# Attention as a pipeline over units: the logits, maximum and Exp of the next unit stand ahead of the mix of this one

## The chip, the core and the metric

The kernel runs on one core of a Trainium2 chip, in one launch. The metric is the device time of that launch in microseconds (us). A core has a matrix engine (TensorE, PE in the profile; its weight loads are PEld), a vector engine (VectorE, DVE), a scalar engine (ScalarE, ACT), GpSimd (POOL) and a sync engine (SP) whose queue issues most of the DMAs. Each engine runs its own instructions in order; an instruction that waits for another engine or for a DMA holds up all that stand behind it on its engine. The same holds for the DMAs in SP's queue.

## What is computed

All in fp32, with S = 2048 tokens, D = 512 channels, F = 1792 hidden channels, 32 heads of 16 channels:

```python
g = sigmoid((x * gate_w).sum(-1, keepdims=True))
# a: attention, each token looks at 8 tokens: itself and those 2, 4, ..., 14 back
q, k, v = heads(x @ wqkv)
logits = einsum("bhsd,bhswd->bhsw", q, k[s - 2*w]) * 16 ** -0.5   # w = 0..7, masked before token 0
a = einsum("bhsw,bhswd->bhsd", softmax(logits), v[s - 2*w]) @ wo
# b: gated feed-forward
b = (gelu(x @ w_gate) * (x @ w_up)) @ w_down
out = g * a + (1 - g) * b
```

## The kernel before

**Halves.** A token looks back in steps of two, so even and odd tokens never meet in the attention. The kernel handles them as two halves, `par` 0 and then `par` 1, each of 1024 tokens. Each half first projects queries and keys (`project` and `project_one` for the first half, `keys` and `key_one` for the second, matmuls on L357 and L506) and values (`values`, L408), and then runs its feed-forward, `ffn(par)`, in 14 steps `f`. After the second feed-forward `out_first` and `finish` multiply the attention's output by `wo` (L1050) and write the result.

**TensorE.** Every fp32 matrix product is three products of rounded high and low parts (`hi`, `lo`), so each result takes three matmuls on a 128x512 tile. `gate_up` computes, for one step `f`, two blocks of gate and up in seven products instead of eight (L778, `p<-S,g` and `p<-A,g`); `down` multiplies the hidden values of two steps with `w_down` (L820). The results stand in eight PSUM banks: four named `acc`, four that rotate under the name `p`. ScalarE copies them out (`s`, `c`, `rt`), computes the Gelu (L870, L886) and rounds to the high parts (`hh`, L796); VectorE adds (L790), multiplies gate by up (L794) and makes the low parts (`hl`, L797) that `down` reads. Weights go through the same split: `combine` (L705) and `operands` (L729) on VectorE for one part, ScalarE and an adding DMA on POOL for the rest; `down_w` makes the parts of `w_down` (L766 for the low part of the first ones).

**The attention runs beside it, on VectorE.** Tokens lie on 128 partitions, eight successive tokens of a half to a partition. A unit is 128 channels (8 heads) of one half: four units in each half, eight in all, counted here from 0 to 7. Units 0 and 1 of a half use the first block of keys, units 2 and 3 the second. The generator `attention()` writes the work of a unit in four parts:

- `load_kq` loads keys and queries into the one buffer `kq` (three DMAs on SP, L553, L554, L550).
- `scores` runs four times: a product of 2048 elements (L569), and a sum over 16 channels (L572). A mask (L576) follows.
- `softmax`: maximum (L583), subtraction (L586), Exp on ScalarE (L588), sum (L589), reciprocal (L591), for the second half a product with the gate (L593), and a multiplication (L595). Beside the maximum an Exp of one element (L584, `ahead`) is issued on ScalarE, whose input is the maximum and whose output nobody reads.
- `mix` loads the values into the one buffer `v` (two DMAs on SP, L553 and L554) and runs four times: a product of 2048 elements (L609) and three additions (L613, L615, L617); after two of them a transpose (L622) and four stores to DRAM (`os`, L624). `channels` later reads these back, and splits them for the product with `wo` (L86 on ScalarE, L87 on VectorE).

There are two `lg` buffers for logits, one `kq`, one `v`, one `prod`, one `m` and one `tb`.

**What sets the order.** `attention()` yields after each instruction with a cost in microseconds. The feed-forward and the projections call `pull(budget)` at fixed places, which takes that many microseconds of work from the generator; a `need(...)` inside it waits until keys or values exist, and `need_o` at the end takes all that is left. The work so taken is given a lower priority. A planner with its own timing of every instruction then chooses the order on each engine, so a change of the generator moves instructions of all engines, also the matmuls. In the order that it makes now, the parts of the units follow one another on VectorE: scores, softmax and mix of one unit, then those of the next, with the feed-forward's instructions in between.

The loads of keys and queries of the next unit stand ahead of `mix`, if its keys are ready. Each half begins with a wait for its keys; the pause `LOAD` (4.0) stands in the generator behind a load that has nothing ahead of it.

Of the kernel before, what the change touches and what calls it, by code (L numbers as in the profile page):

```python
# [10 lines left out]
F32 = mybir.dt.float32  # L11
F32R = mybir.dt.float32r
AF = mybir.ActivationFunctionType
# [3 lines left out]
P = 128  # L17
S, D, F = 2048, 512, 1792
H, DH, W = 32, 16, 8
NT = S // P  # L20
NP = NT // 2
# [6 lines left out]
UC = 128  # L28
UH = UC // DH
# [4 lines left out]
LOAD = 4.0  # L34
# [10 lines left out]
def tile_gated_mix(ctx: ExitStack, tc: tile.TileContext, xt, wqkv, wff, wo, out):  # L45
    nc = tc.nc
    ctx.enter_context(nc.allow_non_contiguous_dma(reason="rows of 512 bytes"))
    pool = ctx.enter_context(tc.tile_pool(name="sb", bufs=1))
# [487 lines left out]
    LG = {}  # L536
# [15 lines left out]
    def load_slots(t, src):  # L552
        nc.sync.dma_start(t[:, :NP - 1], src[:S // 2].rearrange("(p j) d -> p j d", j=NP)[:, 1:])  # L553
        nc.sync.dma_start(t[:, NP - 1:], src[W:].rearrange("(p j) d -> p j d", j=NP))  # L554
# [22 lines left out]
                                op=OP.min)  # L577
        LG[par, u] = lg

    def softmax(par, u):  # L580
        lg = LG[par, u]
        m = pool.tile([P, UH, NP], F32, name="m")
        nc.vector.tensor_reduce(m, lg, axis=AX.X, op=OP.max)  # L583
        nc.scalar.activation(pool.tile([P, 32], F32, name="ahead")[:W, :1], m[:W, 0, :1], AF.Exp, scale=0.0)  # L584
        yield 0.7
        nc.vector.tensor_tensor(lg, lg, m[:, :, :, None].to_broadcast([P, UH, NP, W]), op=OP.subtract)  # L586
        yield 0.7
        nc.scalar.activation(lg, lg, AF.Exp, scale=DH ** -0.5)  # L588
        nc.vector.tensor_reduce(m, lg, axis=AX.X, op=OP.add)  # L589
# [5 lines left out]
        nc.vector.tensor_tensor(lg, lg, m[:, :, :, None].to_broadcast([P, UH, NP, W]), op=OP.mult)  # L595
        yield 0.7

    def mix(par, u, pause):
        lg = LG.pop((par, u))
        hh, c = divmod(u, 2)  # L600
        v = pool.tile([P, 2 * NP - 1, UC], F32, name="v")
        load_slots(v, VS[par, hh][c])
        yield pause
        tb = pool.tile([P, 2, BT * UC], F32, name="tb")
        for jj in range(0, NP, 2):
            if jj % BT == 0:
                o = pool.tile([P, 4, BT, 32], F32, name="o")
            prod = pool.tile([P, 2, W, UC], F32, name="prod")
            paced(nc.vector.tensor_tensor(prod.rearrange("p j w (h d) -> p (j w) h d", d=DH),  # L609
                                          spans(v, jj).rearrange("p j w (h d) -> p j w h d", d=DH),  # L610
                                          two_of(lg, jj)[:, :, :, None].to_broadcast([P, 2 * W, UH, DH]), op=OP.mult))
            yield 2.3
            nc.vector.tensor_tensor(prod[:, :, :4], prod[:, :, :4], prod[:, :, 4:], op=OP.add)  # L613
            yield 1.2
            nc.vector.tensor_tensor(prod[:, :, :2], prod[:, :, :2], prod[:, :, 2:4], op=OP.add)  # L615
            two = [prod[:, :, i].rearrange("p j (b c) -> p b j c", b=4) for i in range(2)]
            nc.vector.tensor_tensor(o[:, :, jj % BT:jj % BT + 2], *two, op=OP.add)  # L617
            yield 1.1

            if jj % BT == BT - 2:  # L620
                t = tb[:, jj // BT]
                nc.vector.transpose(t, o.rearrange("p b t c -> p (b t c)"))  # L622
# [12 lines left out]
    def need(*key):  # L635
        while key not in done:
            yield None

    def attention():
        units = [(0, u) for u in range(NU)] + [(1, u) for u in range(NU)]  # L640
        yield from need(0, 0)
        load_kq(0, 0)
        yield from scores(0, 0)
        yield from need(0, 1)
        scored, mixed = 1, False
        for i, un in enumerate(units):
            if scored == i:
                yield from need(un[0], un[1] // 2 * 2)
                load_kq(*un)
                yield LOAD  # L650
                yield from scores(*un)
                scored += 1
                mixed = False
            yield from need(un[0], 1)
            yield from softmax(*un)


            to = units[scored] if scored < len(units) else None
            ahead = to and (to[0], to[1] // 2 * 2) in done
            if ahead:  # L660
                load_kq(*to)
            yield from mix(*un, LOAD if mixed else 0.0)
            done.add((*un, "o"))
            mixed = not ahead
            if ahead:
                yield from scores(*to)
                scored += 1

    fill = attention()
    credit = [0.0]  # L670

# [567 lines left out]
```

## Time and profile before

| | |
|---|---|
| runs | 600.1, 600.45 and 601.49 us, median 600.45 |
| the profiled execution | 599.87 us |
| its span, first to last instruction | 598.1 us |
| mean granted TensorE clock | 0.998 |
| busy share of TensorE, VectorE, ScalarE, POOL | 99%, 89%, 70%, 15% |
| moved by DMA | 135.68 MB, mean 227 GB/s |

The profiled execution's own time is 1.77 us above its span, and 0.58 us below the median. A share is the engine's busy time over the span; the share of one stage can be another. Rows named by a line, such as L589, carry the line numbers of the kernel before. In the changed kernel the same instructions stand 3 to 13 lines further down (the sum is L592, the table of the Exp belongs to L587).

### The profile page before, as it was taken

How to read it: one execution, taken by the hardware profiler on the slowest of the kernel's cores; microseconds unless marked ns; L12 is line 12 of the kernel's file. 1: busy time of each engine (PE TensorE's matmuls, PEld its weight loads, DVE VectorE, ACT ScalarE, POOL GpSimd, SP SyncE). 2: the span in 40 equal slices, each digit the busy share in tenths (PEclk: the TensorE clock that was granted, in tenths of full speed). 3: DMA queues.
4: the chain of work that ended last, by engine and by line, in shares of the span. 5: the costliest groups of instructions: out<-in, count | busy, mean ns of one | idle time of the engine just before them, and what ended most of it. 6: DMA issues, size and time to landing. Idle time of an engine off the chain costs nothing.

```text
span 598.1 us, 8231 instructions
## 1 busy us (share of the span) xinstructions
PE 591.2 (99%) x2767; PEld 494.3 (83%) x2767; DVE 535.2 (89%) x626; ACT 417.4 (70%) x732; POOL 90.6 (15%) x113
## 2 busy tenths in 40 slices
PE   9999999999999999999999999999999999999997
PEld 7898878888888887888889888888888888888885
DVE  6959899998999969998889998999799979999882
ACT  6664666678877787778777666566877678696722
POOL 0140000111111111103001472111111111121200
PEclk9999999999999999999999999999999999999999
DMA  8795996968687775898899999688968896878815
GB/s 280 255 262 176 295 316 201 274 175 268 187 225 210 228 216 166 228 310 283 268 269 325 243 299 272 203 215 238 257 145 194 239 257 151 219 184 220 109 39 175
DMA packets 90520, 135.68 MB, mean 227 GB/s; under 512 B 8431, under 2 KB 54895, under 8 KB 90478
## 3 DMA queue, kind: packets, MB, share of 16 engines
q1 hardware_dynamic: 70686, 102.98, 52.0%
q0 software_dynamic: 15152, 29.70, 28.0%
q10 hardware_dynamic: 4640, 2.49, 1.4%
q8 instruction: 21, 0.34, 0.2%
q14 instruction: 21, 0.17, 0.1%
HBM read 69.83 MB, written 42.56 MB: 188 GB/s over the span
## 4 chain that ended last, share of the span: by engine, by line
PE 87%; DMA 6%; ACT 4%; DVE 1%; issue 1%; SPq 0%; ACTq 0%; DVEq 0%
PE p L778 41%; PE p L820 13%; PE acc L820 12%; PE p L1050 5%; PE acc L506 5%; PE p L357 2%; PE p L408 2%; PE acc L357 2%; PE acc L1050 2%; PE acc L408 2%; DMA kq<-kq 1%; DMA ks<-hh 1%; PE p L506 1%; DMA vs<-hh 1%; DMA kq<-ks 1%
## 5 line engine op out<-in xcount | busy, mean ns | idle before, releaser
L778 PE MATMUL p<-S,g 128*128 128x512 f32 x672 | 168.7, 389 | 0.7 <-ACT s L783 0.7
L778 PEld LDWEIGHTS p<-S,g 128*128 128x128 f32 x672 | 125.8, 188 | 27.5 <-ACT s L783 1.5
L778 PE MATMUL p<-A,g 128*128 128x512 f32 x504 | 125.1, 389 | 0.4 <-ACT c L886 0.4
L778 PEld LDWEIGHTS p<-A,g 128*128 128x128 f32 x504 | 94.4, 188 | 20.3 <-ACT c L886 0.8
L569 DVE TENSOR_TENSOR prod<-kq 128x2048 f32<-128x2048 f32 x32 | 72.8, 2277 | 4.3 <-DMA kq<-kq 3.6
L609 DVE TENSOR_TENSOR prod<-v,lg 128x2048 f32<-128x2048 f32 x32 | 72.9, 2280 | 0.7
L572 DVE TENSOR_REDUCE lg<-prod 128x128 f32<-128x2048 f32 x32 | 73.0, 2281 | 0.1
L820 PE MATMUL p<-d,hh 128*128 128x512 f32 x224 | 68.6, 390 | 0.4 <-ACT p L814 0.4
L736 POOL DMA_DIRECT2D g<-raw x28 | 24.1, 862 | 255.0 <-ACT g L733 149.6
L820 PE MATMUL acc<-d,hh 128*128 128x512 f32 x224 | 59.9, 389 | 0.0
L789 ACT ACTIVATE c<-p 128x512 f32<-128x512 f32 x56 | 33.5, 597 | 34.1 <-PE p L778 34.0
L820 PEld LDWEIGHTS p<-d,hh 128*128 128x128 f32 x224 | 42.0, 188 | 9.4 <-ACT p L814 0.8
L820 PEld LDWEIGHTS acc<-d,hh 128*128 128x128 f32 x224 | 42.0, 188 | 8.7
L797 DVE TENSOR_TENSOR hl<-c,hh 128x512 fp32r<-128x512 f32 x56 | 38.4, 686 | 6.4 <-ACT hh L796 6.2
L820 PE MATMUL p<-d,hl 128*128 128x512 f32 x112 | 42.9, 389 | 0.0
L794 DVE TENSOR_TENSOR c<-c 128x512 f32<-128x512 f32 x56 | 38.3, 683 | 4.5 <-ACT c L886 4.5
L790 DVE TENSOR_TENSOR c<-c,s 128x512 f32<-128x512 f32 x56 | 38.1, 685 | 3.3 <-ACT c L789 3.3
L783 ACT ACTIVATE s<-p 128x512 f32<-128x512 f32 x56 | 33.0, 594 | 11.3 <-PE p L778 10.1
L769 POOL DMA_DIRECT2D d<-r x23 | 19.7, 856 | 130.3 <-ACT d L768 107.2
L613 DVE TENSOR_TENSOR prod<-prod 128x1024 f32<-128x1024 f32 x32 | 39.0, 1220 | 0.2
L796 ACT ACTIVATE hh<-c 128x512 fp32r<-128x512 f32 x56 | 35.1, 627 | 5.1 <-DVE c L794 4.8
L833 ACT ACTIVATE rt<-p 128x512 f32<-128x512 f32 x48 | 28.5, 596 | 11.9 <-PE p L820 11.6
(215 smaller groups left out, 1004.6 us busy)
## 6 DMA issues: line engine op xcount, KB each, us to landing
g<-raw POOLq DMA_DIRECT2D x28, 512.0 KB, 6.1
raw<-wff SPq DMA_DIRECT2D x42, 256.0 KB, 4.3
ws<-g SPq DMA_DIRECT2D x14, 768.0 KB, 5.5
g<-ws SPq DMA_DIRECT2D x14, 768.0 KB, 7.0
r<-wff SPq DMA_DIRECT2D x28, 256.0 KB, 4.1
d<-r POOLq DMA_DIRECT2D x23, 256.0 KB, 7.1
v<-vs SPq DMA_DIRECT2D x8, 512.0 KB, 7.7
os<-tb SPq DMA_DIRECT2D x64, 64.0 KB, 4.8
```

The source lines that it names most:

```text
L506: LAST[:] = [nc.tensor.matmul(ps, x[:, ts], w, start=(start and kc == i == 0), stop=(kc == 1 and i == 2), skip_group_check=True)]
L569: paced(nc.vector.tensor_tensor(prod, spans(k, jj), q[:, jj:jj + 2, None, :].to_broadcast([P, 2, W, UC]), op=OP.mult))
L572: nc.vector.tensor_reduce(two_of(lg, jj), prod.rearrange("p j w (h d) -> p (j w) h d", d=DH), axis=AX.X, op=OP.add)
L609: paced(nc.vector.tensor_tensor(prod.rearrange("p j w (h d) -> p (j w) h d", d=DH), spans(v, jj).rearrange("p j w (h d) -> p j w h d", d=D ...
L613: nc.vector.tensor_tensor(prod[:, :, :4], prod[:, :, :4], prod[:, :, 4:], op=OP.add)
L778: LAST[:] = [nc.tensor.matmul(ps, w_, a_, start=(start and kc == 0 and n == 0), stop=(kc == 1 and n == 2), skip_group_check=True)]
L790: nc.vector.tensor_tensor(c, c, s, op=OP.add)
L794: nc.vector.tensor_tensor(ge, ge, up, op=OP.mult)
L796: nc.scalar.activation(hh_, ge, AF.Copy)
L797: nc.vector.tensor_tensor(hl_, ge, hh_.bitcast(F32), op=OP.subtract)
L820: LAST[:] = [nc.tensor.matmul(pp, a[:, ts], w, start=(i == 0 and n == 0 and gr == 0), stop=(i == 1 and n == 2), skip_group_check=True)]
L1050: LAST[:] = [nc.tensor.matmul(pa, a, b, start=(first and n == 0), stop=(last and n == 2), skip_group_check=True)]
```

## The change

`softmax` is cut in two. `exps` holds the maximum, the subtraction and the Exp; `shares` holds the sum, the reciprocal, the product with the gate and the multiplication. The one-element Exp `ahead` is gone. The load of the values moves out of `mix` into `load_values`.

The generator's order becomes: load of the values of unit u; scores and `exps` of unit u+1, if its keys are ready; the load of keys and queries of unit u+2, if those are ready; mix of unit u; `shares` of unit u+1. Where the keys of the next unit are not ready, the unit is done by itself as before, with the pause behind its load unless it is the first. This is so for unit 0 and for unit 4, the first units of the two halves. The last unit, 7, has no scores behind it.

```diff
-    def softmax(par, u):
+    def exps(par, u):
         lg = LG[par, u]
         m = pool.tile([P, UH, NP], F32, name="m")
         nc.vector.tensor_reduce(m, lg, axis=AX.X, op=OP.max)
-        nc.scalar.activation(pool.tile([P, 32], F32, name="ahead")[:W, :1], m[:W, 0, :1], AF.Exp, scale=0.0)
         yield 0.7
         nc.vector.tensor_tensor(lg, lg, m[:, :, :, None].to_broadcast([P, UH, NP, W]), op=OP.subtract)
         yield 0.7
         nc.scalar.activation(lg, lg, AF.Exp, scale=DH ** -0.5)
+
+    def shares(par, u):
+        lg = LG[par, u]
+        m = pool.tile([P, UH, NP], F32, name="m")
         nc.vector.tensor_reduce(m, lg, axis=AX.X, op=OP.add)
...
-    def mix(par, u, pause):
-        lg = LG.pop((par, u))
+    VT = {}
+
+    def load_values(par, u):
         hh, c = divmod(u, 2)
-        v = pool.tile([P, 2 * NP - 1, UC], F32, name="v")
+        VT[par, u] = v = pool.tile([P, 2 * NP - 1, UC], F32, name="v")
         load_slots(v, VS[par, hh][c])
-        yield pause
+
+    def mix(par, u):
+        lg, v = LG.pop((par, u)), VT.pop((par, u))
...
     def attention():
         units = [(0, u) for u in range(NU)] + [(1, u) for u in range(NU)]
...
+        def logits(i, wait):
+            if units[i] not in LG:
+                load_kq(*units[i])
+                if wait:
+                    yield LOAD
+            yield from scores(*units[i])
+            yield from exps(*units[i])
+            ready.append(i)
+
+        def share(i):
+            yield from need(units[i][0], 1)
+            yield from shares(*units[i])
+            shared.append(i)
+
         for i, un in enumerate(units):
-            if scored == i:
+            if i not in ready:
                 yield from need(un[0], un[1] // 2 * 2)
...
-            yield from need(un[0], 1)
-            yield from softmax(*un)
...
+                yield from logits(i, i > 0)
+            if i not in shared:
+                yield from share(i)
+            load_values(*un)
+            if keyed(i + 1):
+                yield from logits(i + 1, False)
+                if keyed(i + 2):
+                    load_kq(*units[i + 2])
+            yield from mix(*un)
             done.add((*un, "o"))
-            mixed = not ahead
-            if ahead:
-                yield from scores(*to)
-                scored += 1
+            if i + 1 in ready:
+                yield from share(i + 1)
```

More of the change, by code (lines that the diff above doesn't have):

```diff
@@ L640, in attention, with keyed @@
         units = [(0, u) for u in range(NU)] + [(1, u) for u in range(NU)]
[L641 to L645, printed above, removed]
+        ready, shared = [], []
+        def keyed(i):
+            return i < len(units) and (units[i][0], units[i][1] // 2 * 2) in done
+        def logits(i, wait):
[10 more added lines that the diff above has]
+            shared.append(i)
         for i, un in enumerate(units):
-            if scored == i:
+            if i not in ready:
                 yield from need(un[0], un[1] // 2 * 2)
-                load_kq(*un)
-                yield LOAD
-                yield from scores(*un)
-                scored += 1
-                mixed = False
-            yield from need(un[0], 1)
-            yield from softmax(*un)
-            to = units[scored] if scored < len(units) else None
-            ahead = to and (to[0], to[1] // 2 * 2) in done
-            if ahead:
-                load_kq(*to)
-            yield from mix(*un, LOAD if mixed else 0.0)
+                yield from logits(i, i > 0)
[7 more added lines that the diff above has]
+            yield from mix(*un)
             done.add((*un, "o"))
-            mixed = not ahead
-            if ahead:
-                yield from scores(*to)
-                scored += 1
+            if i + 1 in ready:
+                yield from share(i + 1)
     fill = attention()
```

## The prediction
> **What bounds the kernel now.** I read the page's busy times first, then TensorE's waits, then the chain that ended last.
>
> ```profile
> PE 591.2 (99%) x2767; PEld 494.3 (83%) x2767; DVE 535.2 (89%) x626; ACT 417.4 (70%) x732; POOL 90.6 (15%) x113
> ```
>
> ```profile
> PE p L72 <- DVE warm L69: 1.0, 1, 1.0
> PE p L778 <- ACT s L783: 0.7, 1, 0.7
> PE p L778 <- ACT c L886: 0.4, 1, 0.4
> PE p L820 <- ACT p L814: 0.4, 1, 0.4
> PE p L408 <- ACT p L415: 0.3, 1, 0.3
> ```
>
> ```profile
> 167.00 6.80 PE p L778 x30
> ...
> 591.36 2.73 PE p L1050 x12
> ```
>
> TensorE is busy for 591.2 of 598.1 us. All its waits for others come to 2.8 us, of which 1.0 is the start. The chain's row at 167.00 shows thirty matmuls in 6.80 us, 0.227 each, without a gap, and the last row shows the same rate at the very end (12 in 2.73). The change removes and adds no matmul: both built programs have 2767. So little can be gained: at most the waits behind the start, 1.8 us, that is 0.3%. Much can be lost wherever VectorE, ScalarE or a DMA comes late for a matmul.
>
> How late may they come? I looked at the end, where the last unit's results are split and multiplied with `wo`.
>
> ```profile
> 582.87 0.71 DVE L622 STREAM_TRANSPOSE tb<-o 128x512 f32<-128x512 f32 x1
> ...
> 589.93 0.69 DVE L87 TENSOR_TENSOR hl<-raw,hh 128x512 fp32r<-128x512 f32 x1 [0.55 <-ACT hh L86]
> ```
>
> ```profile
> 591.65 0.39 PE L1050 MATMUL p<-S,hl 128*128 128x512 f32 x1
> ```
>
> The last transpose ends at 583.58, the last low part is ready at 590.62, and the first matmul that reads it starts at 591.65. The attention ends with 1.0 us in hand, so any delay of its last unit beyond that would be paid in full.
>
> **The change part by part.** The orders of both built kernels say what stands where; the durations are rows.
>
> *Exp no longer waited for.* Before, the sum stands directly behind the Exp on VectorE.
>
> ```profile
> DVE m L589 <- ACT lg L588: 7.8, 6, 1.9
> L584 ACT ACTIVATE ahead<-m 8x1 f32<-8x1 f32 x8 | 1.6, 203 | 2.7 <-DVE m L583 2.7
> ```
>
> In six of eight units the new order puts feed-forward work and parts of the mix of the unit before between subtraction and sum, so most of 7.8 us of VectorE's idling goes. Units 0 and 4 keep sum behind Exp; unit 4 loses the advance loading of the Exp table through `ahead`, and its wait grows by about one table load, 1.3. The 1.6 us of `ahead` go from ScalarE. None of this is on TensorE's path: 0 now.
>
> *Fewer dependent neighbours on VectorE.*
>
> ```profile
> 559.58 2.29 DVE L609 TENSOR_TENSOR prod<-v,lg 128x2048 f32<-128x2048 f32 x1
> 561.90 1.22 DVE L613 TENSOR_TENSOR prod<-prod 128x1024 f32<-128x1024 f32 x1
> ```
>
> ```profile
> 493.58 2.29 DVE L609 TENSOR_TENSOR prod<-v,lg 128x2048 f32<-128x2048 f32 x1
> 495.79 1.29 DVE L790 TENSOR_TENSOR c<-c,s 128x512 f32<-128x512 f32 x2
> ```
>
> From start to start the first pair, where the second instruction reads the first one's output, takes 2.32, and the second pair, where it does not, 2.21: 0.11 apart. In the order before, 93 instructions read what the one just ahead wrote; after, 58. That is 35 x 0.11 = 3.9 us less on VectorE, again not on the path. Whether this saving is there matters at the attention's end, below.
>
> *Table loads.* The built programs hold 19 loads of ScalarE's tables before and 20 after. One place changes on the path:
>
> ```profile
> 213.94 1.28 ACT L584 ACT_TABLE_LOAD   x1
> ...
> 216.19 1.28 ACT L886 ACT_TABLE_LOAD   x1
> ...
> 218.10 1.28 ACT L588 ACT_TABLE_LOAD   x1
> ...
> 223.52 1.28 ACT L870 ACT_TABLE_LOAD   x1
> ```
>
> Here a Gelu fell between `ahead` and its Exp, and the four loads made TensorE wait 0.4 for L814. In the new order each Exp directly follows its load. I take -0.4. The waits on L783 and L886 stay: ScalarE's and TensorE's order there is the old one. The extra load, 1.28 beside TensorE, costs 0: ScalarE idles for 30% of the span.
>
> *Scores of unit 1 ahead of mix 0: the one new wait near the path.* Before, the mix of unit 0 began at 76.49 with values loaded long before. After, the order on VectorE from there is: the multiplication L595, one L790, three L705, then the product of unit 1. That needs the queries, whose DMA is issued no earlier, since SP's order up to there is unchanged:
>
> ```profile
> 76.13 0.54 SPq L550 DMA_DIRECT2D kq<-qs  x1
> ```
>
> ```profile
> DMA to landing us min/median/max: 5.8/5.8/5.8
> ```
>
> ```profile
> 75.71 0.69 DVE L595 TENSOR_TENSOR lg<-lg,m 128x512 f32<-128x512 f32 x1
> ...
> 81.04 0.42 DVE L705 TENSOR_TENSOR raw<-raw 128x256 f32<-128x256 f32 x1
> ...
> 88.63 0.95 DVE L729 TENSOR_TENSOR g<-raw,g 128x768 fp32r<-128x768 f32 x1
> ...
> 93.35 1.29 DVE L766 TENSOR_TENSOR d<-r,d 128x512 fp32r<-128x512 f32 x2
> ```
>
> ```profile
> 97.03 0.39 PE L820 MATMUL acc<-d,hh 128*128 128x512 f32 x1
> ...
> 103.38 0.62 PE L820 MATMUL acc<-d,hl 128*128 128x512 f32 x2
> ```
>
> ```profile
> L572 DVE TENSOR_REDUCE lg<-prod 128x128 f32<-128x2048 f32 x32 | 73.0, 2281 | 0.1
> ```
>
> The queries land at 76.13 + 5.8 = 81.9. VectorE is there at about 78.2 (75.71 + 0.7 + 2 x 0.60 + 2 x 0.34, each row less the overlap of 0.08), so it stands still for 3.7, and these instructions queue behind: product and sum (2.3 + 2.2, the size of the L572 row), one L794 (0.60), a product (2.2), L797 (0.60), L729 (0.87), a sum (2.2), L790 (0.60), and the first L766, which ends at 81.9 + 12.2 = 94.1 instead of 94.0. TensorE wants it earlier than before: 12 matmuls fewer stand ahead of its reader, so 97.03 - 12 x 0.227 = 94.3. The margin falls from 3.0 to 0.2. Next is the low part L797 of step 1: second L766 and one L705 (1.2), product (2.2), L790, L794, L705 (1.5), sum (2.2), L794, L705, L797 (1.5) give 102.8, wanted at 103.38 + 8 matmuls (1.8) = 105.2. The margin there is 2.4. With a landing as in the row I take 0.2 us of waiting.
>
> As to the other end of the landing:
>
> ```profile
> DMA to landing us min/median/max: 5.6/6.1/10.0
> ```
>
> These are all seven loads of queries: 5.6 gives 0, and 10.0 is 4.2 later, and costs 4.2 - 0.2 = 4.0. I take the load's own row, since the stores and loads around it keep their order.
>
> *One tighter bank.* Early in the second stage a product takes a `p` bank 0.91 us of TensorE's work after the matmul whose result is copied out of it; before, the shortest such distance in the feed-forward is 1.81.
>
> ```profile
> L833 ACT ACTIVATE rt<-p 128x512 f32<-128x512 f32 x48 | 28.5, 596 | 11.9 <-PE p L820 11.6
> ```
>
> A matmul's record is 0.39, of which 0.16 lies past its 0.227; with the copy's 0.6 that is 0.76, so 0 if ScalarE is free, and 0.6 if one other copy stands ahead. I take 0.2.
>
> *Loads of values.* They move on SP from ahead of the mix to behind the mix of the unit before. Through most units 18 us of the next scores (eight of 2.28) cover them. Without that cover is unit 7:
>
> ```profile
> v<-vs SPq DMA_DIRECT2D x8, 512.0 KB, 7.7
> ```
>
> Between the last product of unit 6 and the first of unit 7 the order has 5.7 us of work, so VectorE stands still for 7.7 + 0.5 - 5.7 = 2.5. Behind it wait low parts for `wo` and the last two L797, and on SP the loads `raw<-os` of the second block of the first half. In unit 3, SP issues the second part of the values behind three loads of value weights, and I bound that stall by 1 to 3 us; it falls into the value projection. Is the attention's end then still in time? VectorE gains 7.8 - 1.3 + 3.9 = 10.4 and loses 3.7 + 2.5 + 3 = 9.2, so it ends 1.2 earlier, and the margin of 1.0 becomes 2.2: 0. Without the 3.9 for dependent neighbours it would end 2.7 later and cost 1.7; I keep the 3.9, since the two pairs above differ by it.
>
> The Trainium skill, "VectorE: DVE Perf Modes", section "The DRAIN you can't avoid", says that a next instruction does not start until the pipe is empty, and that a semaphore between the two costs nothing extra. By this rule the 3.9 would be 0, and the kernel 1.7 slower; this trace does not agree, by the 0.11 between the pairs.
>
> *Sum.* -0.4 + 0.2 + 0.2 = 0.0 against the profiled execution's 599.87. Its span is 598.1, and it ran 0.58 below the median; on the median the forecast is 600.45 + 0.0. The bounds: -1.8 (all waits) to +4.0 + 0.6.
>
> **The rivals.** *Slower:* the queries of unit 1 land late. Stores of keys and queries are issued around that load, and the landing of 10.0 shows the size. It decides from 0.2 us on and turns the verdict at 1.4 late; with 2.5 late the kernel takes 600.45 + 2.3 = 602.8. Against it: SP's order there is unchanged.
>
> *Faster by closing gaps:* all 1.8 us of waits behind the start go, giving 598.7. For it: they are all waits for ScalarE, which loses `ahead`. Against it: the order at L783, L886 and L415 is unchanged.
>
> *Slower at the end:* the dependent neighbours save nothing, the attention's last low part comes 1.7 behind its matmul, and the time is 602.15. For it: the margin of 1.0. Against it: the two pairs of rows.
>
> *Faster since VectorE is the true bound:* then the 10.4 us that it gains count, and the time is 590.05, or 599.25 if its new stalls of 9.2 count as well. Against it: the chain's rows, thirty matmuls at 0.227 each, and TensorE's 2.8 us of waits in all.
>
> The Trainium skill, "Perfetto Trace Analysis", section "Identifying the Most-Contended Engine", would have TensorE judged by its weight loads' busy share, not by its matmuls'. By that rule 83% stands below VectorE's 89%, VectorE comes first, and the case just told is the likely one; the rows of the chain disagree.
>
> *The change doesn't do what it says:* the planner may place sum and Exp together anyway. In the built order it does so in two units of eight only; the time would be 600.45.
>
> **How the numbers follow.** Forecast (no change by more than 0.2%, or 1.2 us, which is about what a measurement of this kernel can tell): 0.48, with a range of its own from 599.3 to 601.6. Change without effect: 0.02. Slower by late queries, or by the same kind of lateness at the tighter bank: 0.28. Slower at the end: 0.05. Gaps closed: 0.14, of which part stays within 1.2. VectorE bound: 0.03. So faster 0.16, same 0.51, slower 0.33. The likeliest time is 600.45, which I give as 600.5. The range for 8 in 10 runs from 598.9, near the case of closed gaps, to 603.4, into the late queries; beyond it lie the bound of 4.6 and the VectorE case.
>
> **What would show it.** Right: waits of VectorE on ACT `lg` fall from 7.8 to under 3; a new wait of some 3.7 on DMA `kq` near 78 and one of some 2.5 on DMA `v` before the last mix; no four table loads between two Gelus; TensorE busy within 1 us of 591.2; the last low part of the attention over 1 us ahead of its matmul. Wrong: a TensorE wait on VectorE's `d`, `hl` or on a copy between 90 and 115; or a wait in `finish` for the attention, which would mean that its end slipped.

## The result, and the profile after

The changed kernel is slower: 606.39 us in the median (605.23 to 610.13) against 600.91 for the kernel before. The ratio is 1.0103, with a 95% interval of 1.0056 to 1.0149. A second comparison, on another occasion, gave 604.61 against 600.81, ratio 1.0072 (1.0049 to 1.0095). So the loss is 5.5 us in the one comparison and 3.8 in the other, and single executions of the changed kernel lie up to 5 us apart. The profiled execution took 606.91, its span is 605.1.

The busy times of the changed kernel, from its page:

```profile
PE 594.9 (98%) x2767; PEld 494.7 (82%) x2767; DVE 532.0 (88%) x626; ACT 416.5 (69%) x725; POOL 90.6 (15%) x113
```

TensorE has the same 2767 matmuls and is busy 3.7 us longer; VectorE is busy 3.2 us less. What TensorE and VectorE of the changed kernel wait for (total, times, longest, in us):

```profile
PE p L791 <- ACT c L802: 2.4, 2, 1.9
PE p L72 <- DVE warm L69: 1.0, 1, 1.0
PE p L791 <- ACT c L899: 0.7, 1, 0.7
PE p L791 <- ACT s L796: 0.7, 1, 0.7
PE p L1063 <- DMA S<-raw: 0.6, 1, 0.6
PE p L791 <- DMA g<-raw: 0.5, 1, 0.5
```

```profile
DVE m L592 <- ACT lg L587: 7.2, 5, 2.3
DVE prod L569 <- DMA kq<-qs: 6.1, 2, 3.5
...
DVE prod L615 <- DMA v<-vs: 2.6, 2, 2.3
```

The first row is new, with a wait of 1.9, and so are the rows for `S<-raw` and `g<-raw`, two adding DMAs that POOL issues. The waits for queries (L569) are new too, and there are two of them, not one.

**Where the time goes.** From the start times of all 2767 matmuls in both timelines one can work out how much later the changed kernel has done the same amount of matmul work. By the clock of the kernel before, that lag is 0.1 us at 80 us, 2.0 at 133, 1.1 at 234 (the gap with the four table loads is gone), 1.3 at 355, 5.9 at 391 and 7.1 at 550, behind a wait for `S<-raw`; and so it stays to the end, which fits the spans (605.1 - 598.1 = 7.0). The largest part, 4.6, falls into 36 us at the start of the second feed-forward. The DMA issues there, on SP, before and after:

```profile
364.36 0.90 SPq L699 DMA_DIRECT2D r<-wff  x2
365.35 0.38 SPq L553 DMA_DIRECT2D kq<-ks  x1
365.79 1.12 SPq L554 DMA_DIRECT2D kq<-ks  x1
366.96 1.19 SPq L550 DMA_DIRECT2D kq<-qs  x1
```

```profile
364.10 0.32 SPq L553 DMA_DIRECT2D kq<-ks  x1
364.47 0.43 SPq L554 DMA_DIRECT2D kq<-ks  x1
...
365.93 0.47 SPq L550 DMA_DIRECT2D kq<-qs  x1
367.50 0.94 SPq L712 DMA_DIRECT2D r<-wff  x2
```

Before, the two loads of `w_down` (`r<-wff`) stand ahead of unit 5's keys and queries; after, behind them. The rows of VectorE and ScalarE of the changed kernel's timeline show both loads landing late:

```profile
366.78 1.29 DVE L779 TENSOR_TENSOR d<-r,d 128x512 fp32r<-128x512 f32 x2
...
378.37 2.29 DVE L569 TENSOR_TENSOR prod<-kq 128x2048 f32<-128x2048 f32 x1 [2.65 <-DMA kq<-qs]
```

```profile
379.33 0.63 ACT L777 ACTIVATE d<-r 128x512 fp32r<-128x512 f32 x1 [3.99 <-DMA r<-wff]
379.87 0.58 ACT L802 ACTIVATE c<-p 128x512 f32<-128x512 f32 x1
```

VectorE stands 2.65 us for the queries. `r` lands 1.0 us behind them; ScalarE stands 3.99 us for it, with the copy `c` of a product bank queued behind. TensorE needs that bank, and its row and the windows around it show what follows:

```profile
380.50 4.61 PE L791 MATMUL p<-A,g 128*128 128x512 f32 x12 [1.87 <-ACT c L802]
```

```profile
375.00:380.00 5.00, 3.63 (x16) 2.57 (x15) 2.32 (x2) 1.01 (x3) 0.00 (x0) 1.00 1.06 324
380.00:385.00 5.00, 4.50 (x13) 3.51 (x14) 5.00 (x6) 3.16 (x6) 0.00 (x0) 0.66 0.38 108
```

A wait of 1.87, and then twelve matmuls in 4.61 instead of the 2.73 to 2.88 that twelve take elsewhere: the granted clock (third number from the end) is 0.66 in the mean of these five microseconds; it is 0.50 from 381.09 to 384.50, as the last section shows. In the kernel before, the same windows have TensorE busy throughout:

```profile
375.00:380.00 5.00, 5.00 (x24) 4.14 (x23) 4.97 (x6) 2.85 (x4) 0.00 (x0) 1.00 0.77 302
380.00:385.00 5.00, 5.00 (x24) 4.14 (x23) 4.93 (x5) 3.23 (x6) 1.13 (x2) 1.00 0.17 34
```

From the starts of the matmuls, the 4.6 us are made up of three parts: 0.8 at 362.68, where a product waits for a copy `c` before either load is late; 2.0 at the wait of 1.87; and 1.7 for 3.41 us at half the clock.

### The profile page after: what moved, and what is told of

The parts are those of the page before. It is cut to its first block, busy times and chain, and to the rows that moved or that the text cites. A ratio compares the mean times of both kernels' runs of the same rounds, so it can differ in the third digit from the quotient of the medians.

```text
span 605.1 us, 8227 instructions
## 1 busy us (share of the span) xinstructions
PE 594.9 (98%) x2767; PEld 494.7 (82%) x2767; DVE 532.0 (88%) x626; ACT 416.5 (69%) x725; POOL 90.6 (15%) x113
## 4 chain that ended last, share of the span: by engine, by line
PE 67%; DMA 13%; issue 10%; DVE 6%; ACT 1%; POOL 1%; SPq 1%; ACTq 0%; POOLq 0%; DVEq 0%
PE p L791 31%; PE p L833 10%; PE acc L833 10%; PE p L1063 5%; PE acc L506 3%; DVE prod L569 2%; PE p L357 2%; DMA vs<-hl 2%; DMA r<-wff 2%; DMA kq<-ks 2%; PE acc L357 2%; PE acc L1063 2%; DVE lg L572 1%; DMA kq<-kq 1%; DMA g<-raw 1%
## 5 line engine op out<-in xcount | busy, mean ns | idle before, releaser
L791 PE MATMUL p<-A,g 128*128 128x512 f32 x504 | 127.8, 394 | 3.6 <-ACT c L802 2.4
L569 DVE TENSOR_TENSOR prod<-kq 128x2048 f32<-128x2048 f32 x32 | 72.9, 2279 | 10.1 <-DMA kq<-qs 6.1
L833 PE MATMUL acc<-d,hh 128*128 128x512 f32 x224 | 58.1, 389 | 0.0
L846 ACT ACTIVATE rt<-p 128x512 f32<-128x512 f32 x48 | 28.0, 594 | 10.4 <-PE p L833 10.3
```

The lines of the kernel that those rows point to most:

```text
L569: paced(nc.vector.tensor_tensor(prod, spans(k, jj), q[:, jj:jj + 2, None, :].to_broadcast([P, 2, W, UC]), op=OP.mult))
L791: LAST[:] = [nc.tensor.matmul(ps, w_, a_, start=(start and kc == 0 and n == 0), stop=(kc == 1 and n == 2), skip_group_check=True)]
L833: LAST[:] = [nc.tensor.matmul(pp, a[:, ts], w, start=(i == 0 and n == 0 and gr == 0), stop=(i == 1 and n == 2), skip_group_check=True)]
```

## The experiments

The second half has two suspects. **L**: `w_down` lands late, being issued late and behind unit 5's loads. **Q**: VectorE stands for unit 5's queries, and everything behind it comes late. For the first half the suspect is unit 1 ahead of the mix of unit 0, **F**. In the kernels below, "behind" means that scores, maximum and Exp of a unit stand behind the mix of the unit before, as before the change. Their line numbers lie a few lines off those of the changed kernel. The growth of the lag is read from the one execution of a kernel that was profiled. In seven of the kernels below that was the fastest of the kernel's executions, up to 2.6 us under their median, so the growth tells the mechanisms apart and need not add up to the median.

**Unit 5 behind.**

```diff
-            if keyed(i + 1):
+            if i in (4,) and keyed(i + 1):
+                load_kq(*units[i + 1])
+            elif keyed(i + 1):
                 yield from logits(i + 1, False)
...
             done.add((*un, "o"))
+            if i in (4,) and i + 1 < len(units) and units[i + 1] in LG:
+                yield from logits(i + 1, False)
```

> The changed kernel, but the scores, maximum and Exp of unit 5 stand behind the mix of unit 4, as before the change; the loads of unit 5's keys and queries stay where the change put them, ahead of the two loads of w_down on SP. All engines' orders are the changed kernel's up to unit 4's last multiplication. Three theories on the 5.5 us by which the changed kernel (606.4) is slower. L: the two loads of w_down (r<-wff) land too late, since they are issued 3 us later, behind unit 5's keys on SP, and land beside them; expected here 605 to 607, ScalarE still waits some 4 us for r<-wff. Q: VectorE stands 2.65 us for unit 5's queries and everything behind it comes late; expected here 602 to 603, with no wait for kq<-qs near 378. F: the loss is made in the first half, where unit 1 stands ahead of the mix of unit 0; expected here 606.

Measured: 603.63 (ratio 1.0039, 1.0025 to 1.0054), between the two forecasts. VectorE's wait near 378 is gone, but ScalarE's wait for `w_down` is not:

```profile
377.39 0.63 ACT L781 ACTIVATE d<-r 128x512 fp32r<-128x512 f32 x1 [4.35 <-DMA r<-wff]
```

TensorE's lag from 355 to 391 grows by 2.0, instead of 4.6. But of the 4.6, 1.7 are the clock and 0.8 come ahead of the late loads, and the second profile of the changed kernel, below, has 1.0 in all; so this run does not show that Q is part of the loss, and L is not ruled out. Later in the same trace VectorE stands 2.85 us for the queries of unit 6, at 433.04, and TensorE's lag does not grow with it (3.4 at 391 and 3.5 at 500): that VectorE stands is not yet a loss.

**Unit 5's load taken away.** `load_kq` returns for unit 5 with the buffer of unit 4. No engine's order changes; three DMAs are gone from SP.

```diff
+        if par and u == 1:
+            LG[par, u] = SAME[0]
+            return
...
+        SAME[:] = [(k, q)]
```

> The changed kernel without the load of keys and queries of unit 5: unit 5 computes its scores from unit 4's, so the output of unit 5 is another, and three DMAs (1.5 MB) are gone; the order of all engines is otherwise the changed kernel's. L: the loads of w_down land in some 8 instead of 11.8 us, ScalarE's wait of 4.0 falls under 1, TensorE's clock stays at 1.00, and the time is 602 to 603. Q: the same time, since VectorE's wait of 2.65 goes too. F: 606.

Measured: 602.68 (1.0027, 1.0014 to 1.0041). With the same order on all engines the lag from 355 to 391 does not grow at all (0.0). So no instruction's place there costs anything by itself; the loads that land late do.

**w_down's low parts earlier.** The two L779 free the buffers `r`. Without their tie to the last matmul in program order (`paced`) they move two instructions of unit 4's scores forward.

```diff
-            paced(nc.vector.tensor_tensor(d[:, 512:], rd, d[:, :512].bitcast(F32), op=OP.subtract))
+            low = nc.vector.tensor_tensor(d[:, 512:], rd, d[:, :512].bitcast(F32), op=OP.subtract)
+            if not par:
+                paced(low)
```

> The changed kernel, but VectorE makes the two low parts of w_down (L779) in the second half two instructions of unit 4's scores earlier, so that the buffers r come free earlier: on SP both loads r<-wff then stand ahead of unit 5's keys and queries instead of behind them. L: r<-wff is there some 6 us earlier, ScalarE does not wait for it, and the time is 602 to 603.5, although VectorE still waits 2 to 5 us for unit 5's queries. Q: the queries are issued no earlier, so VectorE's wait stays or grows, and the time stays at 605.5 to 607. F: 606.

Measured: 606.36 (1.0088, 1.0057 to 1.012). The loads `r<-wff` are issued at 358.12 and nobody waits for them, yet nothing is gained: now the queries are the later ones. Rows of VectorE's timeline and of TensorE's waits:

```profile
378.49 2.29 DVE L569 TENSOR_TENSOR prod<-kq 128x2048 f32<-128x2048 f32 x1 [5.65 <-DMA kq<-qs]
```

```profile
PE acc L835 <- ACT hh L811: 2.9, 1, 2.9
```

The lag grows by 4.8, of which 1.7 are again the clock. ScalarE's high part `hh`, for which TensorE waits, stands behind the late instructions of VectorE, so here Q is enough without L, and L's forecast of 602 to 603.5 was wrong. The planner also reordered matmuls and VectorE's instructions from about 357 us on; what that alone would cost was not run.

**L alone.** In the kernel before, the keys of unit 5 are issued ahead of the softmax of unit 4, and the two `fetch_d` behind them; VectorE keeps unit 5 behind. A dependency that only the planner uses holds the two loads behind the load of the queries (`KEYS5` is the list of those loads).

```diff
+            early_kq = i == NU
+            if early_kq:
+                load_kq(*units[scored])
             yield from softmax(*un)
...
-            if ahead:
+            if ahead and not early_kq:
                 load_kq(*to)
...
-        nc.sync.dma_start(RD[f], wff[f, :, 1024:])
+        ins = nc.sync.dma_start(RD[f], wff[f, :, 1024:])
+        if f in (2, 3) and len(KEYS5) > NU:
+            tc.add_manual_dep(ins.ins, KEYS5[NU].ins.name, mybir.DependencyInfo(mybir.DependencyClass.Sync,
+                              mybir.DependencyReason.SCHED_ONLY), reason="behind")
...
-                at(0 if f != 1 else 5, fetch_d, f + 1)
+                if not par or f not in (1, 2):
+                    at(0 if f != 1 else 5, fetch_d, f + 1)
+                elif f == 2:
+                    at(2, fetch_d, 2)
+                    at(2, fetch_d, 3)
```

> The kernel before, with the two loads of w_down near 364 moved behind the loads of unit 5's keys and queries (and the load g<-ws) on SP; VectorE keeps unit 5 behind the mix of unit 4. If the late loads of w_down alone cost TensorE time: 602 to 605, with a wait of ScalarE for r<-wff of 4 us or more. If only VectorE's standing for the queries costs time: 600.8, as before.

Measured: 603.56 (1.0045, 1.003 to 1.006), and TensorE's lag from 355 to 391 grows by 3.0. VectorE does not stand for the queries in this kernel. SP issues `r` only at 375.34, 2.8 us ahead of its use, so it is the late issue more than the company that makes it late; ScalarE's timeline and TensorE's waits:

```profile
378.12 0.63 ACT L770 ACTIVATE d<-r 128x512 fp32r<-128x512 f32 x1 [6.21 <-DMA r<-wff]
```

```profile
PE acc L826 <- ACT hh L802: 2.7, 1, 2.7
```

So L alone is enough as well.

**Q with the first half as before.** Units 1, 2 and 3 behind (the first diff with `(0, 1, 2)`). The order that follows has `w_down` ahead of unit 5's keys.

> The changed kernel with the whole first half (units 1, 2 and 3) behind the mix of the unit before; the second half pipelined as the change has it. In this order SP has the loads of w_down ahead of unit 5's keys and queries, so what is left in the second half is VectorE's standing for the queries. If that alone costs TensorE time: 603 to 606, with a wait of VectorE for kq<-qs of over 4 us and TensorE waiting 2 to 3 us behind it. If the queries' wait is harmless without late loads of w_down: 600.3 to 602.

Measured: 602.43 (1.0016, 0.9999 to 1.0034), between the two forecasts, and the interval just holds 1. VectorE's wait is the one that Q named, TensorE's a little shorter than its 2 to 3:

```profile
376.56 2.29 DVE L569 TENSOR_TENSOR prod<-kq 128x2048 f32<-128x2048 f32 x1 [4.53 <-DMA kq<-qs]
```

```profile
PE acc L837 <- ACT hh L813: 1.8, 1, 1.8
```

The lag from 355 to 391 grows by 2.1. By the time alone this run would not tell; the waits and the lag do.

**The second half behind.** Units 5, 6 and 7 (the first diff with `(4, 5, 6)`).

> The changed kernel with the whole second half (units 5, 6 and 7) behind the mix of the unit before; the first half as the change has it. If in the second half only unit 5's place matters, as with unit 5 alone put back: 603 to 604. If units 6 and 7 cost something too (the 0.9 us by which TensorE falls back near 547): 602 to 603.

Measured: 603.33 (1.005, 1.0032 to 1.0068), as with unit 5 alone. ScalarE still waits 4.0 for `w_down`, and the lag grows by 2.3 there. Units 6 and 7 don't show.

**Unit 1 behind.** The first diff with `(0,)`.

> The changed kernel, but in the first half the scores, maximum and Exp of unit 1 stand behind the mix of unit 0, as before the change; all units behind are as the change has them, and the order from the second half on is the changed kernel's. L and Q: only the 1.1 to 2.0 us go by which TensorE lags before 230, so 604.5 to 605.5. F: 601 to 602. The wait of 3.5 for unit 1's queries near 78 goes in any case.

Measured: 604.01 (1.0051, 1.0031 to 1.007). The lag from 80 to 133 us grows by 0.1 instead of 1.9; in the second half it still grows by 1.4. The time lies between the forecasts, and by the time alone this kernel can't be told from the changed one in its second comparison (1.0049 to 1.0095). By the lag F is a part of the loss and not the whole.

**Unit 1's load taken away,** in the manner of unit 5's.

> The changed kernel without the load of unit 1's keys and queries: unit 1 computes its scores from those of unit 0, so its output is another, and the wait of 3.5 us near 78 is gone; unit 1 still stands ahead of the mix of unit 0, its scores a few instructions earlier. If the 2.4 us of the first half (which went when unit 1 was put behind the mix) come from the wait for the queries: 602 to 603, with TensorE by 130 within 0.5 us of where the kernel before is. If they come from the place of the scores ahead of the feed-forward's instructions: 604 to 606, with TensorE 1.4 to 2.0 us late by 130.

Measured: 602.74 (1.0042, 1.0027 to 1.0057), in the range named for the wait. But the lag from 80 to 133 still grows by 0.7, between the two forecasts, and the planner moved unit 1's scores. How much of the first half's loss is the wait and how much is the place stays open.

Where the loss falls can be read from the matmuls' starts. The 1.9 of the changed kernel are 0.3 at a Gelu's copy near 86; 0.4 in two steps up to 92; 0.4 at 111, behind a copy `rt`; and 0.8 at 130, where a product waits for the adding DMA `g<-raw`. POOL issues that DMA 8.6 us later than before. Rows of POOL and TensorE after:

```profile
122.64 0.85 POOL L749 DMA_DIRECT2D g<-raw  x1 [7.76 <-PE p L833]
...
129.75 1.20 PE L791 MATMUL p<-A,g 128*128 128x512 f32 x4 [0.50 <-DMA g<-raw]
```

and of POOL before:

```profile
114.00 0.85 POOL L736 DMA_DIRECT2D g<-raw  x1 [0.46 <-DMA v<-vs]
```

The wait at the Gelu's copy is between 0 and 0.9 us in the profiles, with unit 1 in either place, so it is not the change's. The other three come in all six profiles that have this order of the first half (0.3 to 0.5, 0.4, and 0.7 to 1.0, together 1.4 to 1.7), and in none with unit 1 behind.

**The changed kernel again.**

> The changed kernel itself once more, beside the others of this comparison: 605 to 607. In a second profile, either the clock falls again behind the wait at about 378 (then its 1.7 us belong to the loss), or the wait there is shorter than 1 us and the clock stays at 1.00.

Measured: 604.61, a little below the forecast. ScalarE waits 4.55 for `w_down` at 376.01, but no wait of TensorE there is longer than 0.3, it loses only 1.0 from 355 to 391, and the clock stays at 1.00, the second of the two cases. In the first profile SP issued the loads of `w_down` 3.3 us later than here (367.50 against 364.25), while TensorE lagged only 1.4 us more. Thus the loss in the second half is not a fixed sum: the same order gave 4.6, 1.0 and, with unit 1 behind, 1.4.

**Units 1 and 5 behind.** `(0, 4)` in the first diff.

> The changed kernel with units 1 and 5 both behind the mix of the unit before, as before the change; units 2, 3, 6 and 7 stay pipelined. If the two places are the whole loss and add up (2.8 us by putting unit 5 back, 2.4 us by putting unit 1 back), 606.4 - 5.2 = 601.2, that is no difference from the kernel before. If the pipelining of the other four units costs or gains something of its own, the time is off that by more than 1 us: above 602.5 or below 600.

Measured: 603.01 (1.0039, 1.0021 to 1.0057). The two parts did not add up to a return to the time before: `w_down` still stands behind unit 5's keys, ScalarE still waits 4.47 for it, and the lag grows by 1.4. The profiled execution was the fastest of eleven (600.39), so its lags do not account for the loss of the median. With the low parts made earlier as well:

> The changed kernel with units 1 and 5 behind the mix of the unit before, and besides with the two low parts of w_down made two instructions of unit 4's scores earlier, so that both loads r<-wff stand ahead of unit 5's keys and queries on SP. With units 1 and 5 put back alone the time was 603.0, the kernel before 600.8. If those 2.2 are the loads of w_down that land late (ScalarE still waited 4.5 us for them): 600.3 to 601.5, and no wait for r<-wff over 1 us. If they are a cost of the other four pipelined units: 602.5 to 603.5.

Measured: 601.41 (1.0026, 1.0005 to 1.0047). No wait for `r<-wff` is left, the lag from 355 to 391 doesn't grow (0.0), and of the 2.2 us 0.6 are left by the medians; the interval still lies above 1. TensorE waits 0.60 for `S<-raw` near 543 in this kernel, and its lag grows by 0.9 there (last section). With unit 1 behind and unit 5's load taken away:

> The changed kernel with unit 1 behind the mix of unit 0, and without the load of unit 5's keys and queries (unit 5 computes its scores from unit 4's, so its output is another). Both suspected places are then without a wait for queries, while units 2, 3, 5, 6 and 7 stay pipelined. If the loads at these two places are the whole loss: 600.0 to 601.5, no difference from the kernel before. If pipelining costs something elsewhere (TensorE falls back by 0.9 near 547 in some profiles): 601.5 to 603.

Measured: 601.9 against 601.13 (1.0014, 0.9998 to 1.003): 0.4 inside the second range, but the interval holds 1. The growth from 355 to 391 is 0.0; 0.9 come from `S<-raw` near 542. On TensorE, VectorE, ScalarE and POOL the order is the very one of the kernel with unit 1 behind, where the growth is 1.4; only the three DMAs are gone from SP. This is a second pair, beside the changed kernel with and without that load, in which the load alone makes the difference.

**What is left without pipelining.** The kernel before without `ahead` (the diff below), and the changed kernel with every unit behind (`(0, 1, 2, 4, 5, 6)` in the first diff):

```diff
-        nc.scalar.activation(pool.tile([P, 32], F32, name="ahead")[:W, :1], m[:W, 0, :1], AF.Exp, scale=0.0)
```

> The kernel before, with nothing but the one-element Exp (ahead) taken out; VectorE's order and TensorE's stay the same but for a few places. If ahead did its work, VectorE's waits for the Exp grow by about one table load in each of eight units, from 7.8 to some 15 us, and the time stays at 600.5 to 602, as these waits are not on TensorE's path; the four table loads near 214 become two and 0.4 us there go. If the lack of ahead is what slows the changed kernel, 604 or more.

> The changed kernel with scores, maximum and Exp of every unit behind the mix of the unit before. What is left of the change is that ahead is gone and that the values are loaded behind the multiplication of their unit and ahead of the next keys. If the place of the loads of values costs something, over 602; if not, as without ahead alone, 600.5 to 602.

Measured: 600.14 (1.0006, 0.9987 to 1.0024) and 600.15 (0.9998, 0.9981 to 1.0015). Neither the missing `ahead` nor the place of the values' loads, in the order without pipelining, costs anything that can be told. VectorE's wait for the Exp grows to 10.4 in both, not to 15, and in both the lag falls by 0.9 between 210 and 234, where the four table loads were.

**Which units can be pipelined.** Only units 6 and 7, with the low parts earlier (`(0, 1, 2, 4)` in the first diff), twice, and beside it no unit at all:

> The changed kernel with only units 6 and 7 pipelined: units 1, 2, 3 and 5 behind the mix of the unit before, and w_down's low parts made earlier, so that its loads stand ahead of unit 5's keys. With units 2 and 3 pipelined too the time was 601.4 against 600.8. If that rest comes from units 2 and 3: 600.0 to 601.0; if it comes from units 6 and 7: 601.0 to 602.0.

> The kernel with only units 6 and 7 pipelined and w_down's low parts earlier once more, since its gain (ratio 0.9978) is as small as can be told: 599.5 to 600.5 against 600.8 to 601.1 if the gain is real.

> The same with no unit pipelined: the changed kernel with every unit behind the mix of the unit before, and w_down's low parts earlier. If the gain comes from pipelining units 6 and 7: 600.5 to 601.5, a ratio of 1.000. If it comes from the missing one-element Exp and the earlier loads of w_down: as with units 6 and 7 pipelined, a ratio of 0.998.

Measured: 600.14 against 601.13 (0.9978, 0.9963 to 0.9994), then 599.38 against 600.56 (0.9981, 0.9965 to 0.9996), and without any unit 600.19 (0.9995, 0.998 to 1.0009). So this part of the change, with `w_down` kept ahead, beats the kernel before by 0.2%, about what can be told here. Whether the pipelining of units 6 and 7 carries it is not shown: the interval of the run without it holds both answers. The page of the first of these:

```profile
PE 590.7 (99%) x2767; PEld 494.2 (83%) x2767; DVE 533.8 (89%) x626; ACT 414.5 (69%) x723; POOL 90.5 (15%) x113
```

**The table that sorts the kernels** (growth of TensorE's lag from 355 to 391 us, worked out from the timelines as above):

| at the start of the second feed-forward | kernels | growth, us |
|---|---|---|
| neither load waited for long | all units behind, without `ahead`, all behind with low parts earlier, 1 and 5 behind with low parts earlier, 6 and 7 only (twice), both kernels without unit 5's load | 0.0 |
| `w_down` late | unit 5 behind, 1 and 5 behind, second half behind; in the kernel before | 1.4 to 2.3; 3.0 |
| VectorE stands for the queries | low parts earlier (4.8), first half behind (2.1) | 2.1 to 4.8 |
| both | the changed kernel (4.6 and 1.0), unit 1 behind, without unit 1's load (VectorE stands 3.0 there too) | 1.0 to 4.6 |

Of the 4.8 and of the 4.6, 1.7 are the clock. Either late load was enough, and the two don't add up. What fits is one queue: while unit 5's scores come ahead of the mix, the 1.5 MB of keys and queries and `w_down` are wanted at the same time. If the keys go first, `w_down` is late; if `w_down` goes first, the keys are. No run tells the order in the queue from the load on the DMA engines that all queues share, whose busy share is 1.06 from 375 to 380 in the changed kernel.

## Why the prediction was wrong

The forecast was 600.5 with a range to 603.4; the median was 606.4. The sum was -0.4 + 0.2 + 0.2. In the profile the lag grows by 0.1 up to 80, 1.9 in the first half, -0.9 at the table loads, 0.2 up to 355, 4.6 at the start of the second feed-forward and 1.2 near 540 to 550, 7.1 in all. By its own steps:

- **TensorE bounds the kernel, so little can be gained and much lost.** Right. The 3.2 us that VectorE lost in busy time brought nothing, and the case of VectorE as the true bound fell.
- **Scores of unit 1 ahead of mix 0, "the one new wait near the path".** This is the step that failed, by the word "one". The same move stands at the start of the second half: unit 5's queries come directly behind unit 4's multiplication, where mix 4 had covered them. The prediction named unit 4 only for its Exp (+1.3) and did not go through SP's and VectorE's orders there. Nor did it see that a wait of ScalarE for `w_down`, and not only VectorE's for the queries, could hold a product bank. Cost: 1.0 to 4.6 us of lag, against 0 in the sum, and 0.0 again where unit 5's load is taken away.
- **The size of the wait at unit 1.** VectorE's wait was forecast at 3.7 and measured at 3.46, as the row at 82.43 shows, so the landing was right. TensorE was to lose 0.2; in the six profiles with this order its lag grew by 0.8 to 2.1 between 80 and 133. The margins were worked out for two instructions only, L766 and L797, and TensorE waits for neither: its lag stays at 0.9 from 94 to 108. It loses its time elsewhere (the list under "Unit 1's load taken away"), 1.4 to 1.7 us of it in each profile; the largest part is `g<-raw`, an adding DMA for which no margin was worked out.

```profile
82.43 2.29 DVE L569 TENSOR_TENSOR prod<-kq 128x2048 f32<-128x2048 f32 x1 [3.46 <-DMA kq<-qs]
```

- **One tighter bank: 0.2.** Right in kind, and larger. The prediction does not say at what time its place is; the one that fits is at 110.78, where four matmuls (0.91 us) lie between and the second of two copies `rt` ends late. There the lag grows by 0.4, in each of the six profiles.
- **Exp no longer waited for: 7.8 to under 3.** Wrong: 7.2. The new order does put other work between subtraction and sum, but only a few microseconds of it, and the Exp itself starts late on ScalarE, behind a table load. In unit 7 the subtraction starts at 520.07 and the Exp at 524.17:

```profile
520.07 0.67 DVE L585 TENSOR_TENSOR lg<-lg,m 128x512 f32<-128x512 f32 x1
...
524.84 0.69 DVE L592 TENSOR_REDUCE m<-lg 128x64 f32<-128x512 f32 x1 [2.29 <-ACT lg L587]
```

  It cost no time, as the step said: without pipelining the same waits are 10.4, at the time of the kernel before.
- **Dependent neighbours: 3.9 us less on VectorE.** The mechanism holds, a little smaller: its busy time falls from 535.2 to 532.0 with the same 626 instructions, and it is 535.1 in the kernel with every unit behind. Read alone, the rule of the Trainium skill that the prediction weighed against it ("VectorE: DVE Perf Modes", "The DRAIN you can't avoid") would have left it at 535; the same section adds that an instruction which is not held starts earlier.
- **Table loads: -0.4.** Right in kind, and larger: the lag falls by 0.9 there, and by as much with `ahead` alone removed.
- **Loads of values: 0.** Wrong by about 0.9. The stalls of VectorE that it worked out are harmless: unit 3's was 2.34, within the bound of 1 to 3, and unit 7's, forecast at 2.5, was 0.26 (rows below). But the new place of unit 7's load puts it 0.9 us behind the adding DMA `S<-raw`, which then lands late for its matmul (last section).

```profile
315.80 2.29 DVE L615 TENSOR_TENSOR prod<-v,lg 128x2048 f32<-128x2048 f32 x1 [2.34 <-DMA v<-vs]
...
550.11 2.29 DVE L615 TENSOR_TENSOR prod<-v,lg 128x2048 f32<-128x2048 f32 x1 [0.26 <-DMA v<-vs]
```

  TensorE did not wait for the attention's end, as forecast.
- **The rival "slower by late queries"** had the right mechanism in the wrong half, and only one of its two forms. Its 602.8 came closest by luck: it stood for a landing of unit 1's queries 2.5 us late, and they landed as forecast.

## What to carry to other kernels

Moving a consumer ahead of work that used to cover its load must be checked at every place where the pipeline starts anew, here once in each half, and for every other load in the same queue: the one that is pushed back can be the costly one. An engine that stands for a transfer costs what is queued behind it, above all the copy that frees a PSUM bank. Such a loss varies from execution to execution with the landing, so one profile doesn't give its size.

## What the chip showed

**A load lands just behind the one issued ahead of it.** In three profiles with `w_down` behind unit 5's queries, ScalarE's instruction starts 0.96, 1.12 and 1.11 us after VectorE's first product, each right at its landing; the rows of the second profile of the changed kernel:

```profile
374.89 2.29 DVE L569 TENSOR_TENSOR prod<-kq 128x2048 f32<-128x2048 f32 x1 [3.06 <-DMA kq<-qs]
```

```profile
376.01 0.63 ACT L777 ACTIVATE d<-r 128x512 fp32r<-128x512 f32 x1 [4.55 <-DMA r<-wff]
```

SP issued the loads of `w_down` there at 364.25, so 256 KB took over 11 us, against a median of 4.1 for all such loads of that run. The Trainium skill, "DMA: Bandwidth & Descriptors", section "Queues, rings and completion order", says that on each DMA engine the descriptors of one queue are consumed in order; this case agrees.

**A load can make one late that was issued ahead of it on another queue.** Near 543 POOL issues the adding DMA `S<-raw`, which TensorE reads soon after. In the changed kernel SP issues unit 7's values 0.9 us behind it, and it lands after 5.4 us instead of 3.6:

```profile
543.27 0.85 POOL L258 DMA_DIRECT2D S<-raw  x1 [0.19 <-issue]
...
544.15 0.34 SPq L553 DMA_DIRECT2D v<-vs  x1
...
548.72 0.50 PE L1063 MATMUL p<-S,A 128*128 128x512 f32 x1 [0.59 <-DMA S<-raw]
```

Before, no load of values stands near it:

```profile
536.30 0.85 POOL L258 DMA_DIRECT2D S<-raw  x1 [0.19 <-issue]
```

The 19 profiles divide cleanly. In eight the values are issued 0.9 to 1.1 us behind; there `S<-raw` takes 5.3 to 5.6 us, and TensorE waits 0.5 to 0.8 for it and loses 0.8 to 1.1. In the other eleven it takes 3.5 to 3.9 and nobody waits. No run moved this load alone. Some of these kernels lose another 0.3 to 0.6 us near 540, behind copies of ScalarE; why stays open.

**A short wait can cost the clock, and need not.** In the changed kernel TensorE waits 1.87 us, and the granted clock is 0.50 for 3.41 us behind it. With the low parts earlier it waits 2.92, with the same behind it. With `w_down` behind the keys, in the kernel before, it waits 2.68, and the clock stays at 1.00. The traces tell these apart: in all 19 the clock falls a whole number of steps of 3.413 us after its first record (in the changed kernel at 381.09, 110 steps after 5.62). The windows of the three kernels, cut at these steps, in this order:

```profile
377.67:381.09 3.42, 1.55 (x8) 0.96 (x7) 2.72 (x2) 1.75 (x3) 0.00 (x0) 1.00 0.99 356
381.09:384.50 3.41, 3.41 (x10) 2.60 (x9) 3.41 (x4) 1.77 (x4) 0.00 (x0) 0.50 0.23 41
```

```profile
385.95:389.36 3.41, 1.05 (x5) 0.86 (x5) 3.41 (x3) 1.73 (x4) 0.00 (x0) 1.00 1.04 275
389.36:392.78 3.42, 3.42 (x10) 2.64 (x9) 3.42 (x4) 1.99 (x4) 0.86 (x1) 0.50 0.72 199
```

```profile
374.99:378.40 3.41, 2.13 (x10) 1.44 (x8) 0.00 (x0) 0.28 (x1) 0.00 (x0) 1.00 0.68 225
378.40:381.82 3.42, 2.02 (x9) 1.68 (x10) 3.04 (x3) 3.40 (x7) 0.00 (x0) 1.00 0.68 211
```

Counting 0.227 us for each matmul from its start, TensorE is idle for 2.15 us of the step ahead of the fall in the first kernel, and for 2.50 in the second. In the third the wait lies across a border, and 1.44 and 1.53 us fall into the two steps. Over all steps of the 19 traces (most falls are at a kernel's end) the clock fell behind every step with 2.15 us idle or more, and behind none with 2.09 or less. So by these traces the idle part of such a step decides, and not the length of one wait; no run was made to test it. The Trainium skill, "TensorE: Matmul & The Clock Gate", section "Part 1: The HAM clock gate (the "warmup" mystery)", tells of an idle window of about 3.4 us; the length agrees, but a window with 1.26 us of work in it was enough here.
